# Top-32 attention with a gated channel mix: weighted sums, ranks, `norm` and weight magnitudes change places

## The chip, the core and the metric

One core of a Trainium2 chip runs the whole program. The metric is the time of one execution in device microseconds. Five engines work side by side, each through its own queue in program order: TensorE (PE, with PEld for its weight loads), VectorE (DVE), ScalarE (ACT), GpSimd (POOL) and SyncE (SP), which issues the DMAs. They wait for one another through semaphores.

## What is computed

```python
scores = scale * np.matmul(q, k.transpose(0, 1, 3, 2))      # 8 batches, 8 heads, 576 x 576, head size 64
kth = np.partition(scores, -32, axis=-1)[..., -32:-31]
scores = np.where(scores >= kth, scores, -1e9)
attn = np.exp(scores - np.max(scores, axis=-1, keepdims=True))
attn = attn / (np.sum(attn, axis=-1, keepdims=True) + 1e-09)
x = heads_side_by_side(np.matmul(attn, v))                   # 8 x 576 x 512
xk, xr = mu_k * x + (1 - mu_k) * x_prev, mu_r * x + (1 - mu_r) * x_prev   # x_prev: x one token back
k = np.maximum(xk @ w_k, 0.0)                                # 512 x 1024
out = 1 / (1 + np.exp(-(xr @ w_r))) * (k * k @ w_v)
```

Some weights come as 64-bit floats.

## The kernel before

The attention is done in 288 tiles of 128 rows by 576 keys: 8 batches, 4 pairs of heads, 9 tiles each (tiles 0 to 3 of the four pairs, then 4 to 8). A tile passes through several slots, one stage in each, and in slot n every stage works on another tile. A slot is one round of the loop in `pipeline`, and the words of `ORDER` (line 42) say in which order the stages' instructions are written; each engine's queue is that order, with the other engines' instructions left out. Beside these stands `mix`, the matrix products of the channel mix for tokens that are finished. A planner (`Lanes`) hands out its pieces by costs that are written in the code.

The stages that matter here, for slot n:

- `exp` (`exps`, L290): ScalarE writes the exponentials of tile n-3 to PSUM, in the tile `se`.
- `score` (`scores`, L230 and L234): TensorE writes the scores of tile n to PSUM, in the tile `ps`; `keep` (L239): ScalarE copies them to SBUF.
- `weigh` (L367 and L369): TensorE sums the values for a pair of tiles, in 160 of the slots, into columns of `se` behind the exponentials.
- `turn` (`turn_tile`, L309 and L319): TensorE transposes the masked exponentials E of tile n-4; at `et` ScalarE copies them out (L310, L320). `prep` transposes coming queries and keys (L199), `inv` the inverse row sums (L340).
- `c0` to `c6`, `best`, `drop` (L263 to L269), `bounds` (L274): VectorE looks for the 24 largest scores. `count` (L279): ScalarE counts what lies above them, and `below` (L282) is GpSimd's product for the next eight; `eighth` (L909) takes these.
- `thr` (L287): VectorE makes `nine` from the count and from `ranks`, nine constants that lie in the first columns of the tile `ps`; then `mask` (L293) makes E from the scores and the exponentials.
- `norm` (L325): ScalarE adds 1e-9 to the row sums of a finished unit of up to four tiles, in 96 of the slots; `norm2`: the reciprocal (L329) and its spread (L334). `place` (L374 to L379): VectorE multiplies a unit's sums with the inverses, one slot after the last `weigh` of the unit.

In the first slots the 20 blocks of the weights are split too (`weight_block`), one block in two slots: a load (L116), the magnitude (ScalarE, L122), a clamp and two further steps (VectorE, L126, L135, L137), one slot on the powers of two (L139), a rounding (ScalarE, L140) and three steps on GpSimd (L141 to L143). The magnitude and the powers share one buffer, `wmag`, and the magnitude stands at the place `act`, behind the evacuations.

PSUM is watched by tile: an instruction that reads or writes any part of `ps` or `se` waits for the last access of the other engines to that tile, reading or writing. So each `score` waits for `nine` of the slot before, `nine` for `keep`, `weigh` for `exp`, and `mask` for `weigh`, though their columns are apart.

Of the kernel before, what the change touches and what calls it, by code (L numbers as in the profile page):

```python
# [9 lines left out]
F32 = mybir.dt.float32  # L10
F32R = mybir.dt.float32r
I32 = mybir.dt.int32
U32 = mybir.dt.uint32
AF = mybir.ActivationFunctionType
OP = mybir.AluOpType
PSUM = bass.MemoryType.PSUM

B, H, S, D = 8, 8, 576, 64
# [3 lines left out]
HS = S // 2  # L22
MAIN = 512
# [15 lines left out]
PACE, SHARE, PIECE, CAP, MOST = 4.60, 0.74, 1.52, 4.45, 2  # L39
END, HASTE = 36, 1.20  # L40
EXPS, EVAC = 3, (0, 'et')
ORDER = """exp score weigh turn prep inv loads evac keep best0 c0 drop0 c1 best1 c2 drop1 first c3 best2 c4 bounds eighth count norm et high below act late c5 norm2 early thr c6 second place mix mask dve pool weights""".split()


@with_exitstack
def topk_attention_channel_mix(ctx: ExitStack, tc: tile.TileContext, q, k, v, mu_k, mu_r, w_k, w_v, w_r, out):
    nc = tc.nc
# [25 lines left out]
    def open_pools(stack, g, sfx):  # L73
        p = lambda n, bufs, **kw: stack.enter_context(tc.tile_pool(name=n + sfx, bufs=bufs, **kw))
        g.one = p("one", 1)
        g.two = p("two", 2)
        g.three = p("three", 3)
        g.four = p("four", 4)

        scored = p("psS", 1, space=PSUM).tile([128, 2 * 512], F32, name="ps")  # L80
        g.ps, g.ranks = scored[:, 512 - HS:512 + HS], scored[:, :9]


        g.se = p("psE", 1, space=PSUM).tile([128, 2 * 512], F32, name="se")
        g.pe = g.se[:, :S]
        g.sums = g.se[:, S:S + 256], g.se[:, S + 256:S + 320]
        nc.vector.tensor_copy(g.ranks, ranks_i)
        g.turns = 0
        g.ready = range(3 * HP + NFB) if sfx else []
        g.psM = g.psT = p("psM", 4, space=PSUM)  # L90
# [6 lines left out]
    def weight_steps(g, L):  # L97

        blocks = [(w_r, wr, i, 0) for i in range(HP)]
        blocks += [(w_k, wk, i, c) for c in range(0, FF, 512) for i in range(HP)]  # L100
        blocks += [(w_v, wv, i, 0) for i in range(NFB)]
        for src, dst, i, c in blocks:
            weight_block(g, L, src[i * 128:(i + 1) * 128, c:c + 512], *(d[:, i, c:c + 512] for d in dst))
            yield
            yield

    def weight_block(g, L, block, hi, lo):
        val = g.one.tile([128, 512], U32, name="wval")
        valf = val.bitcast(F32)
        if block.dtype == F32:  # L110
            nc.sync.dma_start(valf, block)
            L.at(2, "act", lambda: nc.scalar.activation(hi, valf, AF.Copy))
            L.at(2, "pool", lambda: g.ready.append(nc.gpsimd.tensor_sub(lo, valf, hi.bitcast(F32))))
            return
        st = g.one.tile([128, 512, 2], U32, name="wst")
        nc.sync.dma_start(st.rearrange("p c t -> p (c t)"), block.bitcast(U32))  # L116
        low, high = st[:, :, 0], st[:, :, 1]
        W = Env()

        def magnitude():  # L120
            W.mag = g.one.tile([128, 512], U32, name="wmag")
            nc.scalar.activation(W.mag.bitcast(F32), high.bitcast(F32), AF.Abs)  # L122

        def clamp():
            m = W.mag.bitcast(F32)
            nc.vector.tensor_scalar(m, m, ZERO, None, op0=OP.max)  # L126

        def fine():
            W.fine = g.one.tile([128, 512], F32, name="wfine", tag="rest")
            nc.scalar.activation(W.fine, low, AF.Copy, scale=2.0 ** -52)  # L130

        L.at(2, "act", magnitude)
        L.at(2, "act", fine)
        L.at(2, "dve", clamp)
        L.at(2, "dve", lambda: nc.vector.tensor_scalar(val, W.mag, 3, 0x3FFFFFFF, op0=OP.logical_shift_left,  # L135
                                                       op1=OP.bitwise_and))
        L.at(2, "dve", lambda: nc.vector.scalar_tensor_tensor(val, high, 0xC0000000, val, op0=OP.bitwise_and,  # L137
                                                              op1=OP.bitwise_or))
        L.at(3, "dve", lambda: nc.vector.tensor_scalar(W.mag, val, 0xFF800000, None, op0=OP.bitwise_and))  # L139
        L.at(3, "act", lambda: nc.scalar.activation(hi, valf, AF.Copy))  # L140
        L.at(3, "pool", lambda: nc.gpsimd.tensor_sub(valf, valf, hi.bitcast(F32)))  # L141
        L.at(3, "pool", lambda: nc.gpsimd.tensor_mul(W.fine, W.fine, W.mag.bitcast(F32)))
        L.at(3, "pool", lambda: g.ready.append(nc.gpsimd.tensor_add(lo, valf, W.fine)))  # L143


# [49 lines left out]
    def turn(pt, x):  # L195

        n = x.shape[0]
        for c in range(x.shape[1]):
            nc.tensor.transpose(pt[:, c * n:(c + 1) * n], flat(x[:, c]), ident[:n, :n])  # L199

    def copy_out(fast):
        return nc.vector.tensor_copy if fast else lambda to, x: nc.scalar.activation(to, x, AF.Copy)
# [6 lines left out]
    def turn_q(g, P, j, L, fast=False):  # L209
        n = P.qt[j].shape[1] * 128  # L210
        pt = g.psM.tile([128, MAIN], F32, name="pq", tag="pm")[:, :n]
        turn(pt, P.qt[j])
        P.qs[j] = g.one.tile([128, MAIN], F32, name=f"qs{j}")[:, :n]
        L.at(0, "high", lambda: copy_out(fast)(P.qs[j], pt))

    def turn_rest(g, P, L):
# [8 lines left out]
    def scores(g, P, i):  # L225
        hs = [slice(e * 64, (e + 1) * 64) for e in range(2)]
        if i < 2 * NKC:
            c, j = divmod(i - P.first, 2)
            for e, h in enumerate(hs):
                nc.tensor.matmul(g.ps[:, e * HS:(e + 1) * HS], lhsT=P.qs[j][h, c * 128:(c + 1) * 128], rhs=P.K[h, j], start=True, stop=True)  # L230
        else:
            for j in range(2):
                for e, h in enumerate(hs):
                    nc.tensor.matmul(g.ps[hs[j], e * HS:(e + 1) * HS], lhsT=P.qr[h, hs[j]], rhs=P.K[h, j], start=True, stop=True)  # L234
        return g.ps

    def keep(g, T):
        T.sc = g.four.tile([128, S], F32, name="sc")
        nc.scalar.activation(T.sc, T.ps, AF.Copy)  # L239

    def pick_exact(g, T):
        top = g.four.tile([128, TOPK], F32, name="top")
# [109 lines left out]
    def weigh(g, U, u):  # L352
        P = U.P
        if u == 0:
            U.pa = g.sums[U.u // 2]
        hs = [slice(j * 64, (j + 1) * 64) for j in range(2)]
        if U.u < 2:
            pa = U.pa[:, u * 128:(u + 1) * 128]
            ms = [[U.et[u, j][:, c, :] for j in range(2)] for c in range(NKC)]
            ls = [U.el[u][:, j * 128:(j + 1) * 128] for j in range(2)]  # L360
        else:
            pa = U.pa
            ms = [[U.et[0, 0][:, c, h] for h in hs] for c in range(NKC)]
            ls = [U.el[0][:, h] for h in hs]
        for c in range(NKC):
            for j in range(2):
                nc.tensor.matmul(pa[hs[j]], lhsT=P.v[:, j, c, :], rhs=ms[c][j], start=(c == 0), stop=False)  # L367
        for j in range(2):
            nc.tensor.matmul(pa[hs[j]], lhsT=P.vr[:, j], rhs=ls[j], start=False, stop=True)  # L369

    def place(U):
        xT, hp = U.xT, U.P.hp
        if U.u < 2 and U.P.near:
            nc.vector.tensor_mul(xT[:, hp, 1 + U.u * 256:1 + (U.u + 1) * 256], U.pa, U.ri)  # L374
        elif U.u < 2:
            x = xT[:, hp, 1:1 + MAIN].rearrange("p (q c) -> p c q", c=NKC)[:, 2 * U.u:2 * U.u + 2, :]
            nc.vector.tensor_mul(x, U.pa.rearrange("p (c q) -> p c q", c=2), U.ri.rearrange("p (c q) -> p c q", c=2))
        else:
            nc.vector.tensor_mul(xT[:, hp, 1 + MAIN:], U.pa, U.ri[:, :64])  # L379

# [302 lines left out]
    def new_batch(g):  # L683
        x = g.two.tile([128, HP, 1 + S], F32, name="xT")
        nc.gpsimd.memset(x[:, :, 0:1], 0.0)
        return x

    def pipeline(g):
# [91 lines left out]
        while n < total + 7 or "next" in state or L.busy():  # L780
# [96 lines left out]
            def ranks_(f, r):  # L877
                if C:
                    f(C, r)
# [62 lines left out]
            do.update({f"drop{r}": lambda r=r: ranks_(drop, r) for r in range(2)})  # L942
            for step in ORDER:
                if step in do:
# [7 lines left out]
    with ExitStack() as stack:  # L952
        g = Env()
        open_pools(stack, g, "")
        stack.enter_context(tc.manual_schedule())
        pipeline(g)
# [12 lines left out]
    with tc.If(again > 0):  # L969
        with tc.For_i(0, B, 1) as b, ExitStack() as stack:  # L970
            g = Env()
            open_pools(stack, g, "_again")
            L = Direct()
            xT = new_batch(g)
            rows = out[bass.ds(b, 1)].rearrange("o s d -> (o s) d")
            for hp in range(HP):
                P = Env()
                P.hp = hp
                prep_all(g, P, lambda x: x[bass.ds(b, 1)].rearrange("o h s d -> (o h) s d"), hp, L)
                for i in range(9):  # L980
                    T = Tile_()
                    T.i = i
                    if i % 4 == 0:
                        U = Env()
# [48 lines left out]
```

## Time and profile before

| | before |
|---|---|
| time, median of 3 runs | 1466.51 us (1463.87 to 1469.33) |
| profiled execution, its own time | 1466.39 us |
| span, first to last instruction | 1464.1 us |
| PE busy | 1277.6 us, 87% |
| DVE busy | 1211.5 us, 83% |
| ACT busy | 1170.4 us, 80% |
| POOL busy | 970.5 us, 66% |
| mean granted clock of TensorE | 0.942 |

Busy time is the time in which an engine worked on at least one instruction; waits for semaphores are not in it. The rest of the span is idle, and the profile tells for each idle piece which engine's instruction ended it. The first mask runs at 21 us and the last at 1376 us; the last of the weights' steps on VectorE runs at 253.6 us.

### The profile page before, as it was taken

How to read it: one execution, taken by the hardware profiler on the slowest of the kernel's cores; microseconds unless marked ns; L12 is line 12 of the kernel's file. 1: busy time of each engine (PE TensorE's matmuls, PEld its weight loads, DVE VectorE, ACT ScalarE, POOL GpSimd, SP SyncE). 2: the span in 40 equal slices, each digit the busy share in tenths (PEclk: the TensorE clock that was granted, in tenths of full speed). 3: DMA queues.
4: the chain of work that ended last, by engine and by line, in shares of the span. 5: the costliest groups of instructions: out<-in, count | busy, mean ns of one | idle time of the engine just before them, and what ended most of it. 6: DMA issues, size and time to landing. Idle time of an engine off the chain costs nothing.

```text
span 1464.1 us, 32963 instructions
## 1 busy us (share of the span) xinstructions
PE 1277.6 (87%) x9909; PEld 978.2 (67%) x9909; DVE 1211.5 (83%) x6454; ACT 1170.4 (80%) x2662; POOL 970.5 (66%) x876
## 2 busy tenths in 40 slices
PE   5665766899998999897989999999999898899997
PEld 3444554676776777585767676767767676677786
DVE  6778899887988989898988989898989898889610
ACT  5766777788888988887979888889998897888641
POOL 3656686567556856676767776767676765777673
PEclk9776787999999999999999999999999999999999
DMA  4332223211222122222121212222221222111000
GB/s 98 81 81 69 69 67 85 60 44 37 59 56 49 44 57 63 50 55 51 42 64 39 59 36 62 50 62 53 48 57 45 59 59 64 37 44 42 20 15 21
DMA packets 243817, 78.79 MB, mean 54 GB/s; under 512 B 236464, under 2 KB 236464, under 8 KB 243632
## 3 DMA queue, kind: packets, MB, share of 16 engines
q1 hardware_dynamic: 243632, 76.61, 21.8%
q8 instruction: 82, 1.34, 0.4%
q14 instruction: 103, 0.84, 0.2%
HBM read 67.11 MB, written 9.44 MB: 52 GB/s over the span
## 4 chain that ended last, share of the span: by engine, by line
PE 57%; ACT 21%; DVE 15%; POOL 3%; issue 2%; DMA 2%; SPq 0%; ACTq 0%; DVEq 0%; POOLq 0%
PE se L367 10%; PE pt L309 8%; PE ps L230 6%; PE ph L427 4%; PE ph L428 4%; PE ph L429 4%; ACT sg L279 4%; PE pv L429 3%; PE pv L427 3%; ACT se L290 3%; PE pv L428 3%; DVE cand L263 3%; ACT et L310 3%; ACT xm L403 3%; DVE E L293 2%; PE se L369 2%
## 5 line engine op out<-in xcount | busy, mean ns | idle before, releaser
L282 POOL TENSOR_TENSOR sg<-sc,sg 128x576 f32<-128x576 f32 x288 | 414.4, 1439 | 389.9 <-ACT sg L279 346.4
L263 DVE MAX8 cand<-sc 128x8 f32<-128x82 f32 (+1 forms) x2016 | 466.9, 232 | 1.5 <-ACT sc L239 0.9
L279 ACT ACTIVATE sg<-sc,seen 128x576 f32<-128x576 f32 x288 | 222.7, 773 | 64.9 <-DVE seen L274 60.7
L230 PE MATMUL ps<-K,qs 64*128 64x288 f32 x1024 | 207.2, 483 | 72.6 <-DVE nine L287 64.1
L239 ACT ACTIVATE sc<-ps 128x576 f32<-128x576 f32 x288 | 186.3, 647 | 81.3 <-PE ps L230 72.6
L367 PE MATMUL se<-et,v_in 128*64 128x128 f32 (+1 forms) x2560 | 184.1, 290 | 75.6 <-ACT se L290 70.3
L293 DVE SCALAR_TENSOR_TENSOR E<-sc,seen,se 128x576 f32<-128x576 f32 x288 | 232.5, 807 | 18.9 <-PE se L369 16.8
L367 PEld LDWEIGHTS se<-et,v_in 128*64 128x64 f32 x2560 | 144.1, 149 | 149.5 <-ACT se L290 129.8
L310 ACT ACTIVATE et<-pt 128x512 f32<-128x512 f32 x288 | 170.2, 591 | 72.6 <-PE pt L309 71.4
L290 ACT ACTIVATE se<-sc,seen 128x576 f32<-128x576 f32 x288 | 213.1, 740 | 8.5 <-DVE E L293 8.2
L909 DVE MAX8 top<-sg 128x8 f32<-128x576 f32 x288 | 216.1, 750 | 0.2 <-POOL sg L282 0.2
L309 PE MATMUL pt<-ident,E 128*128 128x128 f32 x1152 | 202.5, 302 | 1.2 <-DVE E L293 1.1
L309 PEld LDWEIGHTS pt<-ident,E 128*128 128x128 f32 x1152 | 130.1, 149 | 81.5 <-issue 37.3
L427 PE MATMUL ph<-xh,wk 128*128 128x256 f32 (+2 forms) x608 | 180.0, 296 | 2.6 <-ACT r L444 1.5
L428 PE MATMUL ph<-xl,wk 128*128 128x256 f32 (+2 forms) x608 | 172.2, 283 | 7.9 <-POOL xl L423 7.9
L230 PEld LDWEIGHTS ps<-K,qs 64*128 64x128 f32 x1024 | 82.5, 196 | 141.7 <-DVE nine L287 44.7
L266 DVE MAX8 top<-cand 128x8 f32<-128x56 f32 x864 | 176.5, 204 | 0.1
L429 PE MATMUL ph<-xh,wk 128*128 128x256 f32 (+2 forms) x608 | 171.0, 281 | 0.0
L427 PE MATMUL pv<-wv,hh 128*128 128x512 f32 (+1 forms) x296 | 125.6, 424 | 1.0 <-ACT et L310 1.0
L428 PEld LDWEIGHTS ph<-xl,wk 128*128 128x128 f32 x608 | 116.4, 191 | 10.3 <-POOL xl L423 10.2
L429 PE MATMUL pv<-wv,hl 128*128 128x512 f32 (+1 forms) x296 | 117.9, 398 | 2.8 <-POOL hl L448 2.7
L427 PEld LDWEIGHTS ph<-xh,wk 128*128 128x128 f32 x608 | 116.1, 191 | 5.5 <-ACT et L310 2.2
(99 smaller groups left out, 2878.9 us busy)
## 6 DMA issues: line engine op xcount, KB each, us to landing
kt<-in_k SPq DMA_DIRECT2D x256, 72.0 KB, 2.3
q_near<-in_q SPq DMA_DIRECT2D x256, 64.0 KB, 2.2
v_in<-in_v SPq DMA_DIRECT2D x128, 128.0 KB, 2.5
out<-eb SPq DMA_DIRECT2D x35, 256.0 KB, 2.1
wst<-in_moe_w_k SPq DMA_DIRECT2D x8, 512.0 KB, 4.1
wst<-in_moe_w_v SPq DMA_DIRECT2D x8, 512.0 KB, 3.7
vr_in<-in_v SPq DMA_DIRECT2D x64, 32.0 KB, 2.4
wst<-in_moe_w_r SPq DMA_DIRECT2D x4, 512.0 KB, 4.2
```

The source lines that it names most:

```text
L230: nc.tensor.matmul(g.ps[:, e * HS:(e + 1) * HS], lhsT=P.qs[j][h, c * 128:(c + 1) * 128], rhs=P.K[h, j], start=True, stop=True)
L263: nc.vector.max(T.cand[:, 8 * i:8 * i + 8], T.sc[:, CUTS[i]:CUTS[i + 1]])
L279: nc.scalar.activation(T.side, T.sc, AF.Sign, bias=T.under, scale=-BELOW, accum_out=T.cnt)
L282: nc.gpsimd.tensor_mul(T.side, T.sc, T.side)
L290: nc.scalar.activation(g.pe, T.sc, AF.Exp, bias=T.nb, scale=SCALE)
L293: nc.vector.scalar_tensor_tensor(T.e, T.sc, T.thr, g.pe, op0=OP.is_ge, op1=OP.mult, accum_out=T.rs)
L309: nc.tensor.transpose(pt[:, c, :], T.e[:, c * 128:(c + 1) * 128], ident)
L367: nc.tensor.matmul(pa[hs[j]], lhsT=P.v[:, j, c, :], rhs=ms[c][j], start=(c == 0), stop=False)
L427: nc.tensor.matmul(ps, lhsT=sh, rhs=mh, start=first, stop=False)
L428: nc.tensor.matmul(ps, lhsT=sh, rhs=ml, start=False, stop=False)
L429: nc.tensor.matmul(ps, lhsT=sl, rhs=mh, start=False, stop=last)
L909: nc.vector.max(M.top[:, 24:32], M.side)
```

## The change

`ORDER` changes in three places: `norm` moves from behind `count` to behind `exp`, `weigh` from behind `score` to behind `keep` (so on TensorE behind `turn`, `prep` and `inv`), and a new place `sign` stands behind `weigh`, ahead of `count`. The weights' magnitude is made at `sign` in place of `act`. The powers of two get a buffer of their own, `wexp`; two query buffers become as small as what they hold. In PSUM the columns of the weighted sums move from the tile `se` to the tile `ps`, one half into each bank behind a half of the scores, and the ranks move from `ps` to `se`, behind the exponentials. No instruction is added or dropped.

```diff
-ORDER = """exp score weigh turn prep inv loads evac keep best0 c0 ... eighth count norm et high below act late ...
+ORDER = """exp norm score turn prep inv loads evac keep weigh sign best0 c0 ... eighth count et high below act late ...
...
-        scored = p("psS", 1, space=PSUM).tile([128, 2 * 512], F32, name="ps")
-        g.ps, g.ranks = scored[:, 512 - HS:512 + HS], scored[:, :9]
-        g.se = p("psE", 1, space=PSUM).tile([128, 2 * 512], F32, name="se")
-        g.pe = g.se[:, :S]
-        g.sums = g.se[:, S:S + 256], g.se[:, S + 256:S + 320]
+        scored = p("psS", 1, space=PSUM).tile([128, 2, 512], F32, name="ps")
+        g.ps = scored[:, :, :HS]
+        g.sums = scored[:, :, HS:HS + 128], scored[:, 0, HS + 128:HS + 192]
+        se = p("psE", 1, space=PSUM).tile([128, 2 * 512], F32, name="se")
+        g.pe, g.ranks = se[:, :S], se[:, S:S + 9]
...
+        def powers():
+            W.exp = g.one.tile([128, 512], U32, name="wexp")
+            nc.vector.tensor_scalar(W.exp, val, 0xFF800000, None, op0=OP.bitwise_and)
-        L.at(2, "act", magnitude)
+        L.at(2, "sign", magnitude)
-        L.at(3, "dve", lambda: nc.vector.tensor_scalar(W.mag, val, 0xFF800000, None, op0=OP.bitwise_and))
+        L.at(3, "dve", powers)
-        L.at(3, "pool", lambda: nc.gpsimd.tensor_mul(W.fine, W.fine, W.mag.bitcast(F32)))
+        L.at(3, "pool", lambda: nc.gpsimd.tensor_mul(W.fine, W.fine, W.exp.bitcast(F32)))
...
-        P.qs[j] = g.one.tile([128, MAIN], F32, name=f"qs{j}")[:, :n]
+        P.qs[j] = g.one.tile([128, n], F32, name=f"qs{j}")
...
-                nc.tensor.matmul(g.ps[:, e * HS:(e + 1) * HS], lhsT=P.qs[j][h, c * 128:(c + 1) * 128], rhs=P.K[h, j], start=True, stop=True)
+                nc.tensor.matmul(g.ps[:, e], lhsT=P.qs[j][h, c * 128:(c + 1) * 128], rhs=P.K[h, j], start=True, stop=True)
...
-        nc.scalar.activation(T.sc, T.ps, AF.Copy)
+        nc.scalar.activation(T.sc.rearrange("p (e k) -> p e k", e=2), T.ps, AF.Copy)
...
-            pa = U.pa[:, u * 128:(u + 1) * 128]
+            pa = U.pa[:, u]
...
-            nc.vector.tensor_mul(xT[:, hp, 1 + U.u * 256:1 + (U.u + 1) * 256], U.pa, U.ri)
+            x = xT[:, hp, 1 + U.u * 256:1 + (U.u + 1) * 256].rearrange("p (u q) -> p u q", u=2)
+            nc.vector.tensor_mul(x, U.pa, U.ri.rearrange("p (u q) -> p u q", u=2))
```

The changed file's line numbers are higher by 4 from the definition of `powers` (its step is L134) to `weigh`, and by 5 behind `place`.

On TensorE, in a slot in the middle of the program that has weighted sums, before (in brackets the semaphores that an instruction waits for, named by the engine or DMA queue that raises them):

```order
L230 MATMUL ps<-K,qs_6087 128x288 [waits DVE_49,Activation_49]
L230 MATMUL ps<-K,qs_6087 128x288
L367 MATMUL se<-et_6078,v_in 64x128 [waits Activation_49]
L367 MATMUL se<-et_6134,v_in 64x128
...
L369 MATMUL se<-el_76,vr_in 64x128 x2
L309 MATMUL pt<-ident,E 128x128 [waits DVE_49,PE_49]
L309 MATMUL pt<-ident,E 128x128 x3
L199 MATMUL pr<-ident,qr_in 128x128 [waits DMAHW1_49,PE_49]
L340 MATMUL px<-ident,rb 128x128 [waits PE_49,Pool_49]
```

The same slot in the changed program:

```order
L234 MATMUL ps<-K,qs_6097 128x288 [waits Activation_49]
L234 MATMUL ps<-K,qs_6097 128x288
L313 MATMUL pt<-ident,E 128x128 [waits DVE_49,Activation_49]
L313 MATMUL pt<-ident,E 128x128 x3
L203 MATMUL pr<-ident,qr_in 128x128 [waits DMAHW1_49,Activation_49]
L344 MATMUL px<-ident,rb 128x128 [waits Activation_49,Pool_49]
L344 MATMUL px<-ident,rb 128x128
L371 MATMUL ps<-et_6088,v_in 64x128 [waits Activation_49]
...
L373 MATMUL ps<-el_76,vr_in 64x128 x2
```

The sums moved behind the three groups of transposes, and write `ps`. Their wait on ScalarE was for `exp` and is now for `keep`; the scores' wait on VectorE is gone in this slot, and in a slot behind a `place` it is for that `place`.

On ScalarE, two slots at the start of the program, the first with a block of weights, the second with `norm` (L325), before:

```order
L239 ACTIVATE sc<-ps 128x576 [waits PE_49,Activation_49,Pool_49]
L279 ACTIVATE sg,cnt<-sc,seen 128x576 [waits DVE_49]
L310 ACTIVATE et_403<-pt 128x512 [waits PE_49]
L202 ACTIVATE qs_412<-pq 128x256 [waits PE_49]
L122 ACTIVATE wmag<-wst 128x512 [waits DMAHW5_49,Pool_49]
L130 ACTIVATE wfine<-wst 128x512 [waits Pool_49]
L290 ACTIVATE se<-sc,seen 128x576 [waits DVE_49]
L239 ACTIVATE sc<-ps 128x576 [waits PE_49,Activation_49]
L279 ACTIVATE sg,cnt<-sc,seen 128x576 [waits DVE_49]
L325 ACTIVATE rs<-rs 128x4
L310 ACTIVATE et_455<-pt 128x512 [waits PE_49]
```

The same two slots in the changed program:

```order
L243 ACTIVATE sc<-ps 128x576 [waits PE_49,Activation_49,Pool_49]
L122 ACTIVATE wmag<-wst 128x512 [waits DMAHW5_49]
L283 ACTIVATE sg,cnt<-sc,seen 128x576 [waits DVE_49]
L314 ACTIVATE et_395<-pt 128x512 [waits PE_49]
L206 ACTIVATE qs_404<-pq 128x256 [waits PE_49]
L130 ACTIVATE wfine<-wst 128x512 [waits Pool_49]
L294 ACTIVATE se<-sc,seen 128x576 [waits DVE_49]
L329 ACTIVATE rs<-rs 128x4
L243 ACTIVATE sc<-ps 128x576 [waits PE_49,Activation_49]
L283 ACTIVATE sg,cnt<-sc,seen 128x576 [waits DVE_49]
L314 ACTIVATE et_458<-pt 128x512 [waits PE_49]
```

The magnitude moved ahead of `count` and of the copies from PSUM, and lost its wait on GpSimd; `norm` moved from behind `count` to behind `exp`.

## Rows read from the trace of the kernel before

**Rows 1.** The page, busy us, share of the span, instructions.

```profile
span 1464.1 us, 32963 instructions
PE 1277.6 (87%) x9909; PEld 978.2 (67%) x9909; DVE 1211.5 (83%) x6454; ACT 1170.4 (80%) x2662; POOL 970.5 (66%) x876
```

**Rows 2.** Stretches: length, busy PE, PEld, DVE, ACT, POOL; clock, DMA share, GB/s.

```profile
21.00:412.00 391.00, 293.27 (x2106) 220.18 (x2107) 332.52 (x1651) 293.27 (x656) 258.05 (x221) 0.83 0.27 65
412.00:1377.00 965.00, 896.76 (x7257) 687.91 (x7256) 859.64 (x4732) 836.14 (x1918) 661.28 (x593) 0.98 0.21 51
```

**Rows 3.** Waits of VectorE, 21 to 412 us: total us, times, longest us.

```profile
DVE wmag L126 <- ACT wmag L122: 21.8, 17, 2.4
DVE rs L329 <- ACT rs L325: 16.5, 23, 3.1
DVE E L293 <- PE se L369: 8.6, 14, 1.5
DVE nine L287 <- ACT sc L239: 6.2, 9, 1.5
```

**Rows 4.** Waits of VectorE, 412 to 1377 us.

```profile
DVE rs L329 <- ACT rs L325: 57.8, 72, 2.4
DVE nine L287 <- ACT sc L239: 35.5, 56, 2.3
DVE E L293 <- PE se L369: 8.2, 8, 1.5
```

**Rows 5.** Waits of TensorE, 412 to 1377 us.

```profile
PE se L367 <- ACT se L290: 44.0, 37, 2.4
PE ps L230 <- DVE nine L287: 8.2, 6, 2.1
```

**Rows 6.** Timeline at 219 us, a `place`: start us, duration us, instruction.

```profile
219.33 0.41 DVE L374 TENSOR_TENSOR xT<-se,ri 128x256 f32<-128x256 f32 x1
```

**Rows 7.** Timeline, a slot at 776 us; in brackets idle us and its releaser.

```profile
776.00 0.76 PE L230 MATMUL ps<-K,qs 64*128 64x288 f32 x4
...
778.23 1.09 PE L367 MATMUL se<-et,v_in 128*64 128x128 f32 x16 [1.47 <-ACT se L290]
778.59 0.64 ACT L239 ACTIVATE sc<-ps 128x576 f32<-128x576 f32 x1
...
779.47 0.66 PE L309 MATMUL pt<-ident,E 128*128 128x128 f32 x4
...
779.97 0.38 PE L199 MATMUL pq<-ident,q_near 128*128 128x128 f32 x2
```

**Rows 8.** Timeline, a slot at 845 us.

```profile
845.49 0.76 PE L230 MATMUL ps<-K,qs 64*128 64x288 f32 x4
...
847.79 0.63 ACT L239 ACTIVATE sc<-ps 128x576 f32<-128x576 f32 x1
...
847.90 1.74 PE L367 MATMUL se<-et,v_in 128*64 128x128 f32 x16 [1.66 <-ACT se L290]
...
850.00 1.12 PE L309 MATMUL pt<-ident,E 128*128 128x128 f32 x4
...
851.55 0.42 PE L340 MATMUL px<-ident,rb 128*128 128x128 f32 x2
```

**Rows 9.** Timelines at 49 and 225 us: GpSimd's product and a clamp.

```profile
48.77 1.42 POOL L282 TENSOR_TENSOR sg<-sc,sg 128x576 f32<-128x576 f32 x1
...
50.25 0.43 DVE L126 TENSOR_SCALAR wmag<-wmag 128x512 f32<-128x512 f32 x1 [1.71 <-ACT wmag L122]
...
224.82 1.43 POOL L282 TENSOR_TENSOR sg<-sc,sg 128x576 f32<-128x576 f32 x1
...
224.91 1.62 DVE L126 TENSOR_SCALAR wmag<-wmag 128x512 f32<-128x512 f32 x1 [0.45 <-ACT wmag L122]
```

**Rows 10.** The line that loads the weights, L116: its DMAs' time to landing.

```profile
DMA to landing us min/median/max: 3.4/4.0/4.7
```

More of the change, by code (lines that the diff above doesn't have):

```diff
@@ L41 @@
 EXPS, EVAC = 3, (0, 'et')
-ORDER = """exp score weigh turn prep inv loads evac keep best0 c0 drop0 c1 best1 c2 drop1 first c3 best2 c4 bounds eighth count norm et high below act late c5 norm2 early thr c6 second place mix mask dve pool weights""".split()
+ORDER = """exp norm score turn prep inv loads evac keep weigh sign best0 c0 drop0 c1 best1 c2 drop1 first c3 best2 c4 bounds eighth count et high below act late c5 norm2 early thr c6 second place mix mask dve pool weights""".split()
 @with_exitstack
@@ L233, in scores @@
                 for e, h in enumerate(hs):
-                    nc.tensor.matmul(g.ps[hs[j], e * HS:(e + 1) * HS], lhsT=P.qr[h, hs[j]], rhs=P.K[h, j], start=True, stop=True)
+                    nc.tensor.matmul(g.ps[hs[j], e], lhsT=P.qr[h, hs[j]], rhs=P.K[h, j], start=True, stop=True)
         return g.ps
@@ L373, in place @@
         if U.u < 2 and U.P.near:
-            nc.vector.tensor_mul(xT[:, hp, 1 + U.u * 256:1 + (U.u + 1) * 256], U.pa, U.ri)
+            x = xT[:, hp, 1 + U.u * 256:1 + (U.u + 1) * 256].rearrange("p (u q) -> p u q", u=2)
+            nc.vector.tensor_mul(x, U.pa, U.ri.rearrange("p (u q) -> p u q", u=2))
         elif U.u < 2:
             x = xT[:, hp, 1:1 + MAIN].rearrange("p (q c) -> p c q", c=NKC)[:, 2 * U.u:2 * U.u + 2, :]
-            nc.vector.tensor_mul(x, U.pa.rearrange("p (c q) -> p c q", c=2), U.ri.rearrange("p (c q) -> p c q", c=2))
+            nc.vector.tensor_mul(x, U.pa, U.ri.rearrange("p (c q) -> p c q", c=2))
         else:
```

## The prediction

> **What bounds the kernel now.** I read the busy shares first, then the same shares by stretch, then who waited for whom in each stretch, and last single slots in the order of time. TensorE is busy 1277.6 us of a span of 1464.1 and VectorE 1211.5 [rows 1]: no engine is full, so the loss lies in how they wait for each other. By stretch the kernel has two faces [rows 2]. From 21 to 412 us the weights are split beside the first tiles. There VectorE is the fullest, 332.5 of 391 us (85%), TensorE and ScalarE stand at 293 (75%) each. From 412 to 1377 us TensorE is the fullest, 896.8 of 965 us (93%), ahead of VectorE (859.6, 89%) and ScalarE (836, 87%). The rest is head and tail, where no tile is in work; the change hardly touches them.
>
> The reader should see what VectorE waits for. In the first stretch it is idle 391 - 332.5 = 58.5 us, and four waits make 53.1 of that: the clamp for the weights' magnitude 21.8, the reciprocal for `norm` 16.5, the mask for the weighted sums 8.6, `nine` for `keep` 6.2 [rows 3]. In the second stretch it is idle 105.4 us, and 101.5 of that are the last three [rows 4]. TensorE is idle 68.2 us there, and 44.0 of that, in 37 pieces, are weighted sums waiting for `exp`; 8.2 more are scores waiting for `nine` [rows 5]. Neither pair passes data to the other: they meet because sums and exponentials share a tile of PSUM, and scores and ranks another.
>
> **The change part by part.** The number of instructions and their shapes stay, so every term is a wait.
>
> *Sums with the scores, ranks with the exponentials.* `nine` now follows `exp` in place of `keep`, and ScalarE does `exp` first in a slot, so `nine` loses a wait and gets an easier one. The mask no longer follows the sums. The scores of the next slot no longer follow `nine`; in 96 of 288 slots they follow `place`, which stands two short steps behind `nine` and ahead of the mask. The transposes right behind the scores need that mask anyway, so I cost this at nothing; if that cover were gone it would cost the 0.41 us of a `place` [rows 6] and a part of the candidate step ahead of it in each, 39 us and more.
>
> *`weigh` behind `turn`, `prep` and `inv`.* The sums now wait for `keep`, which ScalarE does after `exp`. TensorE has the transposes to do meanwhile, and they are what `exp`'s wait used to hold up. Two slots show the bounds. At 847.90 the sums start after 1.66 us of idling; scores were done at 846.25, turn to `inv` take from 850.00 to 851.97, that is 1.97 us [rows 8]. In the new order these run from 846.25 to 848.22, `keep` ends at 848.42, the sums take their 2.10 us and end at 850.56: 1.41 us sooner. At 778.23 the sums start after 1.47 us; scores were done at 776.76, turn and prep take 0.88 [rows 7]. In the new order they are over at 777.64, but `keep` ends only at 779.23, since an evacuation lies between it and `exp`; the sums end at about 780.5 instead of 780.35, 0.15 us later. So a waiting sum gives between -0.15 and +1.41 us. I take 0.5, below their middle of 0.63, since `keep` gets later in just the slots in which ScalarE is late: 37 x 0.5 = 18 us in the second stretch, with ends of -6 and 52. On top, transposes that run before the sums are evacuated earlier, and what ScalarE has queued behind that copy starts earlier. I give this no term of its own.
>
> The Trainium skill ("PSUM — Partial Sum Buffer", section on bank collisions) says that two engines may not be in one bank at once, even at different columns. This trace agrees: the 44.0 us are a wait between disjoint columns [rows 5]. By that rule the change doesn't remove a conflict but swaps partners, and the new one, `keep`, comes later than `exp`; this is the slower rival below.
>
> *`norm` behind `exp`.* In place of standing behind `count`, where ScalarE had to wait for VectorE's bounds, the addition runs right behind `exp`, which waits for the same mask as it does. VectorE has all its candidate steps ahead of the reciprocal, so the wait goes to about nothing: 16.5 us in the first stretch, 57.8 in the second. It adds its step to what stands ahead of `keep` in 96 slots, behind which `weigh` now waits.
>
> *Magnitude early, powers in a buffer of their own.* The wait of 21.8 us should go, but what lies in that idle time? At 50.25 the clamp starts after 1.71 us of idling and takes 0.43; GpSimd's product had just ended (48.77 + 1.42 = 50.19). At 224.91 the clamp ran beside the same product and took 1.62 [rows 9]. So a clamp moved up by 1.7 us runs where GpSimd works, and gives back about 1.62 - 0.43 = 1.2. The bounds: all 21.8 gained where GpSimd is quiet, and where each of 20 clamps and the two steps behind it are stretched by 1.2: 20 x 3 x 1.2 - 21.8 = 50 us lost. I take half the wait, 11 us, since only some of it lies beside the product. The Trainium skill ("GPSIMD Engine Reference", section 1, Specifications) says that GpSimd shares its SBUF interfaces with VectorE; this trace agrees (0.43 against 1.62). The magnitude also needs its weights sooner: the load takes 3.4 to 4.7 us [rows 10] and is issued more than a slot ahead, with 1464.1 / 288 = 5.1 us to a slot; I cost that at nothing.
>
> **The sum.** First stretch: 16.5 + 8.6 + 6.2 + 11 = 42 us of VectorE's idle time go. Were all of it gained, VectorE would be 332.5 / 349 = 95% busy; in the second stretch no engine gets above 93%. I take 91%: 332.5 / 0.91 = 365, a gain of 26 us. Second stretch: 18 us at TensorE, and of VectorE's 101.5 us only 4, since that engine is not the one that is full. Together 48 us. The profiled execution took 1466.39 us (its span and 2.3 us around it), 0.1 us from the median of 1466.51, so no correction: 1466.4 - 48 = 1418 us.
>
> **The rivals.**
> *TensorE keeps its pace (A).* In the second stretch the idle time merely moves from `exp` to `keep`, as the slot at 778 shows; against it speaks the slot at 847. Only the first stretch's 26 us are left: 1440 us.
> *The coupling was all there was (B).* With `nine`, reciprocal and mask free, VectorE and TensorE may run apart by a slot, and both stretches get denser than anything shown: 95% of VectorE in the first (350, a gain of 41) and 97% of TensorE in the second (925, a gain of 40): 1385 us. For it speaks that nearly all of VectorE's idle time has a name that the change removes; against it that each engine also waits for ScalarE, at 87%.
> *`keep` is the worse partner (C).* There are 160 weighted sums, most of which don't wait now. If `keep` ended 1.3 us behind the scores, twice its own 0.64 [rows 7], because an evacuation or `norm` stands ahead of it, and turn and prep covered 0.88, each would lose 0.42: 67 us, and 1466.4 - 48 + 67 = 1485. It decides from 48 / 160 = 0.3 us per sum on. Against it: in the slot at 847 `keep` directly follows `exp`, and the sums would wait 0.2 us [rows 8].
> *The waits only change names (D).* The clamps are stretched by what they no longer wait, the sums wait for `keep` as long as for `exp` in both stretches, and VectorE's freed waits turn up ahead of the next candidates: 1466 us, within a few us. For it speaks the slot at 778; against it, that the reciprocal's 74 us (16.5 + 57.8) hang on nothing but an order on ScalarE.
>
> **Chances and range.** Forecast 0.53, A 0.20, B 0.12, D 0.09, C 0.06. What this kernel's measurement can tell from no change is about 0.5%, 7 us. Forecast, A and B are faster by more: 0.85; D is the same: 0.09; C slower: 0.06. The range runs from 1388 (short of B's end) to 1456 (beyond A, with some of its 26 us lost to stretched clamps); C, D and the deep end of B lie outside.
>
> **What would show it.** Right: the reciprocal's wait near nothing; `nine` waits for neither `keep` nor anything else; VectorE busy about 90% in the first stretch; the sums' wait now ended by `keep` and under 30 us in the second; clamps without a wait, but most of them slower than 0.43 us. Wrong: TensorE's idle time ahead of the sums as long as before or longer (A, C), a new wait of candidates for `keep` on VectorE as large as those removed (D), or the magnitude waiting for its load, which would hold `count` and all behind it on ScalarE.

## The result and the profile after

The changed kernel takes 1448.51 us (median of 4 runs, 1448.05 to 1450.08), the one before 1466.01 us (1463.87 to 1469.33): a ratio of 0.988 (0.986 to 0.990), 17.5 us faster. The forecast was 48 us faster; of the times named beforehand, rival A's 1440 us is the nearest.

The page of the changed kernel, first its span and busy times:

```profile
span 1448.2 us, 32903 instructions
PE 1289.6 (89%) x9909; PEld 971.8 (67%) x9909; DVE 1205.7 (83%) x6454; ACT 1160.8 (80%) x2662; POOL 968.2 (67%) x876
```

To compare stretches I cut each run at the same work, the start of the 73rd mask and of the last. Before, these lie at 412.5 and 1376.4 us, after at 391.2 and 1360.8: the first stretch, counted from the span's start, gained 21.3 us (forecast 26), the second grew from 963.9 to 969.6 us (forecast a gain of 22). The tail is 87.7 and 87.4. So the first stretch fell short by some 5 us, and the second by 27.7. The same view by stretch as in [rows 2], of the changed kernel:

```profile
21.00:391.20 370.20, 285.01 (x2078) 209.01 (x2078) 341.87 (x1657) 289.50 (x653) 261.54 (x220) 0.87 0.28 68
391.20:1360.80 969.60, 915.45 (x7279) 691.78 (x7278) 842.50 (x4728) 830.33 (x1921) 655.69 (x593) 0.98 0.21 51
```

VectorE is now 92% busy in the first stretch (forecast 91%). In the second its busy share fell, 842.5 of 969.6 us, 87%. Its waits there, which answer to [rows 4]:

```profile
DVE xT L379 <- PE ps L373: 40.2, 23, 3.0
DVE top L914 <- POOL sg L286: 27.5, 53, 0.8
DVE xT L379 <- POOL xT L690: 16.2, 5, 4.0
DVE xT L379 <- ACT sc L243: 12.7, 16, 1.1
DVE eb L485 <- PE pv L434: 11.1, 9, 2.0
DVE nine L291 <- ACT se L294: 6.7, 15, 0.9
DVE rs L333 <- ACT rs L329: 3.4, 6, 0.7
```

The three waits of 101.5 us shrank as forecast, `nine` to 6.7 and the reciprocal to 3.4, and the mask's is not in the list any more. New ones took their place. Ahead of `place` (L379) stand 69.1 us: for late sums (L373), for `keep` (L243), and for something that the prediction did not see, a clearing on GpSimd (L690). Another 27.5 stand ahead of `eighth` (L914), for GpSimd's product. TensorE's waits, which answer to [rows 5]:

```profile
PE ps L371 <- ACT sc L243: 20.5, 27, 2.0
PE ps L234 <- DVE xT L379: 18.4, 7, 5.6
```

The sums wait 20.5 us in place of 44.0, but the scores wait 18.4 us for `place`, in only 7 pieces. One of them in the order of time (the line of TensorE is cut off at two of its four matmuls, where the window ends):

```profile
744.99 0.10 POOL L690 MEMSET xT<- 128x4 f32 x1
745.13 0.43 DVE L379 TENSOR_TENSOR xT<-ps,ri 128x256 f32<-128x256 f32 x1 [3.97 <-POOL xT L690]
745.47 0.81 DVE L297 SCALAR_TENSOR_TENSOR E<-sc,seen,se 128x576 f32<-128x576 f32 x1
...
745.61 0.85 PE L234 MATMUL ps<-K,qs 64*128 64x288 f32 x2 [5.61 <-DVE xT L379]
```

Read from the top: a tenth of a microsecond of clearing stands at the end of GpSimd's queue; `place` waits 3.97 us for it, the mask stands behind `place` on VectorE, and the next scores wait for `place` because its sums lie in their tile. TensorE idles 5.61 us. The buffer is cleared once for each of the 8 batches. All 8 times `place` starts right behind the clearing, after a wait of 1.2 to 4.0 us, and in 6 of them TensorE then idles ahead of the scores, 0.9 to 5.9 us.

### The profile page after: what moved, and what is told of

It reads as the page before. It is cut to its first block, busy times and chain, and to the rows that moved or that the text cites. A ratio compares the mean times of both kernels' runs of the same rounds, so it can differ in the third digit from the quotient of the medians.

```text
span 1448.2 us, 32903 instructions
## 1 busy us (share of the span) xinstructions
PE 1289.6 (89%) x9909; PEld 971.8 (67%) x9909; DVE 1205.7 (83%) x6454; ACT 1160.8 (80%) x2662; POOL 968.2 (67%) x876
## 4 chain that ended last, share of the span: by engine, by line
PE 59%; DVE 19%; ACT 13%; POOL 5%; issue 2%; DMA 1%; SPq 0%; ACTq 0%; DVEq 0%; POOLq 0%
PE ps L371 8%; PE ps L234 8%; PE pt L313 6%; PE ph L432 5%; PE ph L433 4%; PE ph L434 4%; PE pv L432 4%; PE pv L434 4%; PE pv L433 4%; DVE cand L267 3%; DVE E L297 3%; ACT sc L243 3%; ACT sg L283 2%; DVE top L914 2%; ACT xm L408 2%
## 5 line engine op out<-in xcount | busy, mean ns | idle before, releaser
L286 POOL TENSOR_TENSOR sg<-sc,sg 128x576 f32<-128x576 f32 x288 | 420.8, 1461 | 410.3 <-ACT sg L283 363.7
L243 ACT ACTIVATE sc<-ps 128x576 f32<-128x576 f32 x288 | 186.3, 647 | 128.1 <-PE ps L234 104.6
L234 PE MATMUL ps<-K,qs 64*128 64x288 f32 x1024 | 206.4, 482 | 57.8 <-DVE xT L379 42.6
L914 DVE MAX8 top<-sg 128x8 f32<-128x576 f32 x288 | 216.6, 752 | 33.4 <-POOL sg L286 32.6
L313 PEld LDWEIGHTS pt<-ident,E 128*128 128x128 f32 x1152 | 127.1, 146 | 152.6 <-issue 101.0
L313 PE MATMUL pt<-ident,E 128*128 128x128 f32 x1152 | 197.5, 297 | 32.6 <-DVE E L297 29.2
L371 PE MATMUL ps<-et,v_in 128*64 128x128 f32 (+1 forms) x2560 | 178.5, 286 | 27.4 <-ACT sc L243 26.4
L371 PEld LDWEIGHTS ps<-et,v_in 128*64 128x64 f32 x2560 | 140.2, 147 | 59.6 <-ACT sc L243 51.6
L433 PEld LDWEIGHTS ph<-xl,wk 128*128 128x128 f32 x608 | 116.6, 192 | 10.7 <-POOL xl L428 10.5
```

Of the source, the lines that this page charges most:

```text
L234: nc.tensor.matmul(g.ps[:, e], lhsT=P.qs[j][h, c * 128:(c + 1) * 128], rhs=P.K[h, j], start=True, stop=True)
L243: nc.scalar.activation(T.sc.rearrange("p (e k) -> p e k", e=2), T.ps, AF.Copy)
L286: nc.gpsimd.tensor_mul(T.side, T.sc, T.side)
L313: nc.tensor.transpose(pt[:, c, :], T.e[:, c * 128:(c + 1) * 128], ident)
L433: nc.tensor.matmul(ps, lhsT=sh, rhs=ml, start=False, stop=False)
L914: nc.vector.max(M.top[:, 24:32], M.side)
```

## The experiments

"First" and "second" are the two stretches, cut at the 73rd and the last mask, from each run's own trace; before 412.5 and 963.9, changed kernel 391.2 and 969.6 us. Ratios are to the kernel before, measured beside each run, with 95% intervals. Each stretch is read from one profiled execution. Executions of the kernel before differ by some 6 us and those of e9 by 9, so a difference of a few microseconds between two rows is not clear of noise.

| run | median us | ratio | first | second |
|---|---|---|---|---|
| e1_norm | 1459.15 | 0.995 (0.993 to 0.997) | 407.4 | 960.0 |
| e2_magnitude | 1457.80 | 0.994 (0.993 to 0.996) | 404.0 | 963.8 |
| e3_place_first | 1480.42 | 1.010 (1.008 to 1.012) | 398.1 | 991.3 |
| e4_weigh_score | 1461.65 | 0.996 (0.995 to 0.998) | 395.7 | 977.6 |
| e5_keep_first | 1527.65 | 1.042 (1.040 to 1.044) | 402.9 | 1034.7 |
| e6_old_banks | 1445.24 | 0.986 (0.984 to 0.987) | 400.2 | 955.8 |
| e8_weigh8 | 1457.07 | 0.994 (0.992 to 0.996) | 393.5 | 972.1 |
| e9_early_memset | 1437.68 | 0.980 (0.977 to 0.983) | 389.1 | 961.1 |
| e13_memset_only | 1465.36 | 1.000 (0.999 to 1.001) | 410.5 | 963.8 |
| e10_more_dve | 1504.96 | 1.026 (1.023 to 1.028) | 422.5 | 993.9 |
| e11_more_pe | 1501.66 | 1.024 (1.022 to 1.026) | 417.0 | 991.5 |
| e12_weigh_last | 1418.27 | 0.967 (0.965 to 0.969) | 387.8 | 938.9 |

**One part alone.** `norm` moved in the kernel before:

```diff
-exp score weigh turn ... count norm et high
+exp norm score weigh turn ... count et high
```

> The kernel before with one edit: the addition of norm stands right behind exp. Both theories below hold that VectorE's freed waits are slack once TensorE is the fullest engine, so the second stretch (from the 73rd mask to the last, 964 us before) should stay within 6 us, with the reciprocal's wait of 57.8 us gone to under 5. In the first stretch (to the 73rd mask, 412.5 us) VectorE is the fullest, and the 16.5 us of this wait should give 6 to 12 us. Total 1452 to 1462 us. If the second stretch gains over 12 us, VectorE's waits there were no slack, and both theories need mending.

5.1 us in the first stretch, just short of the 6 to 12 expected, and 3.9 in the second. Where did the second stretch's 57.8 us go? Two waits of VectorE there:

```profile
DVE nine L287 <- ACT sc L239: 72.8, 112, 2.0
...
DVE rs L329 <- ACT rs L325: 3.9, 8, 0.6
```

Of the reciprocal's wait 53.9 us went, and `nine`, the very next instruction in VectorE's queue, took 37.3 of them over: 72.8 us in place of 35.5. It waits for `keep`, on the same ScalarE.

The magnitude alone (the diff's lines on `sign`, `powers` and the query buffers):

> The kernel before with one edit: the magnitude made at the early place ahead of count, the powers of two in their own buffer, the query buffers cut to size. Only the first stretch has weights: by the prediction's 11 of 21.8 us at VectorE, some 5 to 9 us there, second stretch within 5 us; total 1456 to 1463 us. The clamp's mean should rise above its 828 ns, since it now runs beside GpSimd's product. If the first stretch gains over 14 us, the magnitude is the main part of the first stretch's 21.4 us and norm and the shared banks are not.

8.5 us in the first stretch, the upper end, nothing in the second. The clamp's line in this run, then the step behind it, in the kernel before (L135) and in this run (L139); the three times are shortest, median and longest in ns:

```profile
L126 DVE TENSOR_SCALAR wmag<-wmag x20: 427/790/1503, 15.2 to 236.7; 128x512 f32<-128x512 f32 x20
```

```profile
L135 DVE TENSOR_SCALAR wval<-wmag x20: 426/428/1470, 17.2 to 248.9; 128x512 uint32<-128x512 uint32 x20
```

```profile
L139 DVE TENSOR_SCALAR wval<-wmag x20: 426/1392/1471, 15.6 to 237.4; 128x512 uint32<-128x512 uint32 x20
```

The clamp's waits fell from 24.3 to 0.9 us, and its mean hardly rose, from 828 to 851 ns. The price was paid one step later: the step behind the clamp, mostly alone before, now mostly runs beside GpSimd. Clamp and the two steps behind it take 62.5 us in place of 48.9. So 23.4 us less waiting and 13.6 us more work leave 9.8, near the 8.5 measured.

**Is it `place`, or the partner of the sums?** Two theories for the second stretch, each with a run that should have gained:

```diff
-exp norm score turn ... c6 second place mix
+exp norm place score turn ... c6 second mix
```

> The changed kernel with place written ahead of the scores of its slot, at the start of VectorE's slot, where its sums have long been done. Theory P (the gain of the second stretch was eaten by place, which now shares a bank with scores and keep: VectorE waits 69 us ahead of it there): these waits fall to under 15 us and the second stretch (969.6 us) gains 15 to 40 us: total 1410 to 1433 us. Theory K (TensorE's wait ahead of the sums moved from exp to keep one for one, and VectorE's waits are slack): place's waits fall as well, but the second stretch stays within 6 us; total 1442 to 1454 us, and TensorE's wait for keep stays at about 20 us of idle time, with prep and inv holding on for some 108 us from start to next start.

```diff
-exp norm score turn prep inv loads evac keep weigh sign
+score turn prep inv loads keep weigh exp norm evac sign
```

> The changed kernel with exp, norm and the evacuations written behind keep and weigh, so that ScalarE copies the scores first and the sums wait for a copy that waits only for the scores. Theory K: TensorE's wait ahead of the sums falls by more than half, from 42 us of extra time ahead of weigh, and the second stretch (969.6 us) gains 15 to 35 us: total 1413 to 1433 us. Theory P: place's ties stay, exp comes later by one copy, and the second stretch stays within 6 us or loses: total 1442 to 1460 us.

Both lost, and each opened another wait on VectorE. `place` at the head of the slot waits 74.2 us in the second stretch for its inverse (L349), which ScalarE copies late in the slot before. `keep` ahead of `exp` did cut the sums' wait, from 20.5 to 8.1 us, but `exp` and `norm` came late:

```profile
DVE nine L291 <- ACT se L294: 117.2, 109, 3.4
DVE rs L333 <- ACT rs L329: 53.2, 52, 2.8
```

So neither decides between the theories. The second speaks against one thing that theory K and the prediction shared, though, that waits on VectorE in the second stretch are slack: with these the stretch is 65 us longer. It moves the evacuations back too, so this is not shown by it alone; e10 below tests it.

**The banks against the order.** The changed order with the tiles `ps` and `se` laid out as before (and with `place` in its old form of two dimensions):

```diff
+        g.ps, g.ranks = scored[:, 512 - HS:512 + HS], scored[:, :9]
...
+        g.sums = g.se[:, S:S + 256], g.se[:, S + 256:S + 320]
```

> The changed order with the PSUM layout of before: weigh behind keep, norm and magnitude early, but the sums share their tile with the exponentials and the ranks with the scores. By the runs so far norm gives 5.1 us in the first stretch and 3.9 in the second, the magnitude 8.5 and 0.1; what is left of the change, moving weigh and exchanging the banks, gives 7.7 in the first and costs 9.7 in the second. Theory P (the exchange of banks costs: place waits for keep, for the late sums of tile 8 and for a memset): the second stretch falls from 969.6 to 945 to 960 us. Theory W (moving the sums behind the transposes costs, whatever the bank, for the next copies and evacuations come late): it stays at 965 to 980 us.

Theory P's side: the second stretch falls to 955.8 us. Exchanging the banks costs 13.8 us there and gives 9.0 in the first. The waits of the second stretch show what the order alone does, VectorE first:

```profile
DVE E L297 <- PE se L373: 64.2, 75, 1.7
DVE nine L291 <- ACT sc L243: 38.9, 71, 1.9
```

```profile
PE se L371 <- ACT se L294: 9.2, 18, 1.3
```

With `weigh` behind the transposes the sums' wait for `exp` falls from 44.0 to 9.2 us, and the mask, which shares a tile with them here, waits 64.2 us for late sums in place of 8.2. If the parts add up, the move itself gave 960.0 - 0.1 - 955.8 = 4.1 us, a remainder over several runs and no more than two executions of one kernel differ by.

The other way round, the changed banks with the sums right behind the scores:

```diff
-exp norm score turn prep inv loads evac keep weigh sign
+exp norm score weigh turn prep inv loads evac keep sign
```

> The changed kernel with weigh written right behind the scores again, so the banks are exchanged and the sums wait for neither exp nor keep, while keep waits for the sums. Theory W: with the sums at their old place the second stretch is back at 955 to 962 us or better, since TensorE's wait ahead of the sums is gone altogether. Theory P: place is bound to keep and to the memset as before, only the wait for tile 8's late sums goes; the second stretch stays at 962 to 972 us. In the first stretch keep, and with it VectorE's candidates, come 1.3 us later in a slot with sums; it should lose some of its 21 us.

977.6 us, which neither theory had: with these banks the move of `weigh` gives 8.0 us. With the sums ahead of it `keep` comes late, and the candidates wait 28.8 us for it (0.9 in the changed kernel).

Only tile 8's sums early:

```diff
+            def weigh8_():
+                if W and W.i == 8:
+                    weigh(g, W.U, 0)
...
-                if W and (W.i % 2 or W.i == 8):
+                if W and W.i % 2:
...
-exp norm score turn
+exp norm score weigh8 turn
```

> The changed kernel with only the sums of tile 8 (32 of 160) right behind the scores, so that place of the unit before need not wait for them at the end of its slot (40.2 us in 23 waits in the second stretch). Theory P: that wait goes and the second stretch gains 8 to 20 us on 969.6. Theory W: VectorE's wait there is slack; within 5 us.

The 40.2 us are gone, and theory P is wrong on them: `place` waits 43.8 us for `keep` instead (12.7 before that), and the stretch is 2.5 us longer, within the noise.

```profile
DVE xT L379 <- ACT sc L243: 43.8, 39, 1.9
```

**The clearing.** The buffer is taken and cleared one slot sooner:

```diff
+                if W and ends(W) and W.U.P.b not in xT:
+                    ...
+                    xT[b] = new_batch(g)
                 T = tiles.get(n - 6)
                 if T and ends(T):
                     U = T.U
-                    if U.P.b not in xT:
-                        ...
```

> The changed kernel with a batch's activation buffer taken and its first column cleared one slot sooner. In the changed kernel place, written with three dimensions, waits for that memset at the end of GpSimd's queue (18.9 us in 7 waits, 16.2 in 5 in the second stretch), which it did not before. If these waits are on the path, the second stretch gains 6 to 16 us; if VectorE's waits at place are slack, within 4 us.

10.7 us by the spans (1448.2 to 1437.5): 2.1 in the first stretch and 8.5 in the second. The four executions of this run lie 9 us apart (1432.83 to 1441.83), all of them under the changed kernel's fastest by 6 us or more, so the 8.5 is good to some 4 us. In the second stretch the wait for L690 fell from 16.2 to 0.8 us, and the scores' wait for `place` from 18.4 to 6.3:

```profile
PE ps L234 <- DVE xT L379: 6.3, 5, 2.4
```

With the buffer, what GpSimd does ahead of taking it (the `...` of the cut) comes a slot sooner too, and that might be the gain. The control is therefore the same edit in the kernel before, whose `place` is written with two dimensions and does not wait for the clearing. In the kernel before, the first `place` of a batch had ended before the clearing of its buffer began, in all 8 batches; one of them:

```profile
1244.45 0.41 DVE L374 TENSOR_TENSOR xT<-se,ri 128x256 f32<-128x256 f32 x1
...
1246.30 0.10 POOL L685 MEMSET xT<- 128x4 f32 x1
```

> The kernel before with the activation buffer taken and cleared one slot sooner, as in the run that gained 10.7 us on the changed kernel. Theory Z (the changed kernel's place waits for that clearing, and the kernel before's does not): nothing changes here, second stretch 961 to 967 us, total within 5 us of before. Rival (taking the buffer sooner helps by itself, since it pulls GpSimd's remaining steps of the batch forward, and the wait was not the cost): 6 to 12 us faster here as well.

Nothing (1.000, 0.999 to 1.001): it is the wait, not the earlier buffer.

**How full are the engines?** More work that leaves the result as it is, in the kernel before: the last candidate step three times, or two of four transposes twice.

```diff
+            for _ in range(3 if i == NCH - 1 else 1):
...
-        for c in range(NKC):
+        for c in (0, 1, 2, 3, 2, 3):
```

> The kernel before with VectorE's last candidate step done three times in place of once: the same result, two more instructions of some 0.15 us from start to next start in each of 288 slots, 22 us in the first stretch and 65 us in the second. The prediction held VectorE's waits in the second stretch for slack behind TensorE: then the second stretch grows by less than 25 us. If VectorE is as much a bound there as TensorE, it grows by 45 us or more. In the first stretch, where VectorE is the fullest, by 15 to 25 us.

> The kernel before with two of a tile's four transposes done twice: the same result, two more instructions of some 0.126 us from start to next start in each slot, 18 us in the first stretch and 54 us in the second. If TensorE is the bound of the second stretch, as the prediction held, it grows by 40 us or more there; if TensorE's waits leave room, by less than 25. In the first stretch, where TensorE is 75% busy, by less than 10 us.

The second stretch of each, in the columns of [rows 2]; VectorE first:

```profile
422.50:1416.40 993.90, 903.40 (x7243) 691.62 (x7242) 934.13 (x5154) 844.50 (x1916) 660.97 (x593) 0.98 0.21 50
```

```profile
417.00:1408.50 991.50, 936.56 (x7678) 733.37 (x7676) 860.18 (x4728) 835.85 (x1918) 658.22 (x593) 0.99 0.21 50
```

VectorE took 76 us more work (934.1 against 858.6 in the kernel before) and the stretch grew by 30.0: 40%. TensorE took 41 us more busy time, or 48 if its transposes are counted from start to start (155.8 against 107.7), and it grew by 27.6: 57 to 67%. Both results lie between the two cases that their expectations named: neither engine is the bound alone, and neither is slack. In the first stretch VectorE was expected to pass 15 to 25 us on and passed on 10.0, though its busy time there grew by 27 (from 333.0 to 359.9): even where it is the fullest, its waits took up more than half.

**Sums last.** With the early clearing, the sums written behind the channel mix, while the planner's cost for them stays where it was:

```diff
+            def sums():
+                if W and (W.i % 2 or W.i == 8):
+                    weigh(g, W.U, W.i // 2 % 2)
...
-second place mix mask
+second place mix sums mask
```

> The changed kernel with the early clearing, and with the weighted sums written behind the pieces of the channel mix, the last work of TensorE in a slot, so that keep has long been done when they start. If the wait ahead of the sums (21.8 us of idle time in the second stretch, some 42 us with what hides in the pipeline) is what still holds that stretch, it falls from 961 to 930 to 950 us and the total to 1408 to 1428 us, the fastest so far. If the wait is slack, or the sums of tile 8, which now wait for a place at the end of VectorE's slot, cost as much, it stays at 955 to 975 us.

The fastest: 1418.27 us, the second stretch at 938.9. Its waits there, VectorE's at `place`, then TensorE's at the sums:

```profile
DVE xT L379 <- ACT sc L243: 25.8, 41, 1.3
```

```profile
PE ps L371 <- ACT sc L243: 12.3, 9, 1.7
```

`place` no longer waits for late sums (40.9 us in e9), and the sums wait for `keep` in 9 pieces in place of 27: TensorE has its transposes and the mix to do between the scores and the sums.

## Why the prediction was wrong

**The signs of being right came, and the gain did not.** The waits that were to go went: the reciprocal's is near nothing, `nine` waits 6.7 us in place of 35.5, the sums wait for `keep` and under 30 us, VectorE is 92% busy in the first stretch, 18 of 20 clamps take longer than 0.43 us. None of the signs of being wrong came. What failed is that other waits took their place, at instructions that the signs did not name: `place`, and the scores behind it.

**First stretch: about right.** 26 us were forecast and 21.3 measured, at 92% busy. VectorE's idle time fell by 30 us (from 58.5 to 28.3) and not by 42, and its work grew by 9 (from 333.0 to 341.9): clamp and the two steps behind it take 64.1 us in place of 48.9. Alone, `norm` gave 5.1 and the magnitude 8.5; by subtraction the rest, 7.7, is the banks and the sums.

**Second stretch.** The two steps below make up the 27.7 us: 13.8 and, by subtraction, 18 - 4.1 = 13.9.

**Failed step 1: "The transposes right behind the scores need that mask anyway, so I cost this at nothing."** The exchange of banks costs 13.8 us of the second stretch (e6), and 8.5 of these, good to some 4, are the clearing (e9, with e13 as control). The sum looked at where `place` stands in the queue and not at what `place` itself waits for. Its new form with three dimensions touches the same buffer as the clearing, and in the built program it waits for it although their columns are apart; the scores and the mask then inherit the wait. That the three dimensions make the difference is argued: they are all that changed in how `place` touches this buffer. What the other 5 us are is open: `place` waits for late sums or for `keep`, and taking the one away (e8) brought the other.

**Failed step 2: "a waiting sum gives between -0.15 and +1.41 us. I take 0.5 ... 18 us".** The move gave about 4 us with the old banks and 8 with the new, not 18. The two slots from which the price was taken did little harm: the same working over all 36 waits of over 0.15 us ahead of sums right behind scores, in the trace of the kernel before, gives from -0.16 to 1.51 us, 0.38 in the mean and 14 us in all. So the rest of the miss was not in the slots chosen. What the price left out is who waits for sums that come later: with the old banks the mask (64.2 us in place of 8.2, e6), with the new ones `place` (40.2). That these waits ate the gain is argued, not shown. And part of the wait for `exp` became one for `keep`, as rival A had it. Idle time ahead of the sums fell by 23.5 us (44.0 to 20.5), but part of the rest hides, since TensorE's records overlap: from the start of one matmul to that of the next, summed over the second stretch, scores take 151.7 us in place of 193.8, and `prep` and `inv` 115.2 in place of 66.2. Some 7 of these 49 us more stand ahead of scores that wait for `place`; the rest of the time moved from one place to the other. The Trainium skill ("PSUM — Partial Sum Buffer", section on bank collisions) says that two engines collide in one bank, in the same partitions, also at different addresses; the runs agree in that the sums, beside the scores now, wait 20.5 us for `keep`, which reads other columns. More was to be had from the sums: e12 gained 22.2 us of the second stretch over e9. It took away `place`'s wait for late sums and nearly half of the sums' wait for `keep` (12.3 us in place of 21.8) together, so how much belongs to which is open.

**Third term: right in size by luck.** VectorE's freed waits of the second stretch, those of the reciprocal, `nine` and the mask, were put at 4 us because they were held for slack; e1, which frees the reciprocal's alone, gave 3.9. But they are not slack: 76 us more work on VectorE cost 30 (e10). They gave little because waits behind them in the same queue took them over, 72.8 us at `nine` in e1, the 69.1 at `place` in the changed kernel. That was rival D, for one stretch, and at `place` where D had said the candidates.

**The slower rival** did not decide: with all sums back behind the scores the second stretch is 8.0 us longer (e4), with those of tile 8 alone no shorter (e8).

## What to carry to other kernels

A wait that is removed is worth what the next wait in the same queue leaves of it; list that one before giving the removed one a price, and take the idle time that is left as the sign of success, not the waits that went. When a buffer is moved to another bank, follow every instruction that touches the moved columns, in the built program: what it waits for now, what stands behind it, and who waits for that. Work whose inputs are ready early and whose result is wanted late belongs behind the work that can fill a wait, not at the place where its new partner is just finishing: here that gave 22.2 us (e12 over e9).

## What the runs showed of the hardware

A clearing of 0.10 us cost TensorE 5.61 us in one slot only through the queues.

VectorE's steps took longer beside GpSimd's, as in [rows 9]. In the changed kernel no clamp reached the 1.62 us of those rows; the slowest of 20 took 0.99. But the step behind it, which took 0.43 to 0.44 us in each of the 14 cases in which it ran alone before, ran beside a TENSOR_TENSOR of GpSimd in 19 of 20 cases and took 1.07 to 1.63 us there. The clamp and this step in the changed kernel:

```profile
L126 DVE TENSOR_SCALAR wmag<-wmag x20: 423/888/993, 15.5 to 235.2; 128x512 f32<-128x512 f32 x20
```

```profile
L139 DVE TENSOR_SCALAR wval<-wmag x20: 428/1469/1628, 15.9 to 235.9; 128x512 uint32<-128x512 uint32 x20
```
